# Attention scores of eight heads on eight tiles of TensorE, with the softmax, its buffers and the sums of states laid out again

## The chip, the cores and the metric

The kernel runs on one core of a Trainium2 chip. The metric is the device time of one execution in microseconds; smaller is better. A core has TensorE (PE in the rows; its weight loads are PEld), VectorE (DVE), ScalarE (ACT) and GpSimd (POOL), each of which works off its own list of instructions in order. SyncE (SP) issues most of the DMA transfers, POOL some; a queue also issues in order, so a transfer that has to wait holds up those behind it.

## The reference

```python
def _attn_ref(x, state):                     # x (8, 8, 512, 64), state (8, 8, 32, 64)
    scores = scale * np.matmul(x, state.transpose(0, 1, 3, 2))
    a = softmax(scores)                      # over the 32 states; written out, with 1e-09 in the sum
    xread = np.matmul(a, state)
    scores2 = scale * np.matmul(state, x.transpose(0, 1, 3, 2))
    a2 = softmax(scores2)                    # over the 512 tokens
    sread = np.matmul(a2, x)
    return np.concatenate([xread, sread], axis=2)

x = attn_out.transpose(0, 2, 1, 3).reshape(8 * 544, 512)
h = x @ w_in; x = (h * sigmoid(1.702 * h)) @ w_out        # 512 -> 2048 -> 512
h = x @ w_in2; out = (h * np.cos(h)) @ w_out2             # 512 -> 2048 -> 512
```

Per batch and head, 32 states and 512 tokens are scored against each other. One matrix of scores serves two softmaxes: over the states (its result reads the states for each token) and over the tokens (its result reads the tokens for each state). The 544 rows of each of the eight batches then go through two MLPs.

## The kernel before

**The first MLP.** It is worked in passes t = 0 to 6, then the tail t = 8 (the 256 rows of the states of all batches), then t = 7; a pass is one batch of 512 tokens, in 16 steps c. A step does on TensorE, in this order: `hidden(t, c)` (L499, or L507 with 12 matmuls in pass 0 and the tail; for batches 1 to 7 it is 6 matmuls against the products of states and weights, tiles `swt`), `second` of the step two before (L556, 12 matmuls into `py`), and then the pieces put into this step. ScalarE makes `t1` (Silu, L528) and `gh` (L517), VectorE `gl` (L519).

**Pieces.** While pass t runs, the attention of batch t+1 is done in pieces, and in pass 5 also the part of batch 0 that reads tokens for the states. The tuples `parts`, `first_parts` and `first_s` say which piece stands in which step; `plan` puts them into `todo`. A batch has two groups g of four heads. `scores` (L373): four matmuls of 32 columns over all 128 rows, in one bank of `ps_a`, called `psA`; the state operand `sblk` has zeros for the other head of each pair. `max_n`, `exp_n`, `norm_n` (softmax over states), `max_s`, `exp_s`, `norm_s` (over tokens), `turn_s` (four transposes into `psB`, copied to `a2T`), `sread` (16 small matmuls of `a2T` against `xN`, into `psC`), `place_s` (eight transposes on VectorE into `xs`). `ps_a` has two banks for `psA`, `psB`, `psC` and `psS`. The token tiles have one buffer per tag: one `xN_t`, two `xT_t`.

**Products of states and weights.** `sw_piece` makes them for two batches at a time: 6 matmuls into `psS` (L308), a copy to `swo` on ScalarE (L312), the remainder on VectorE (L313), and two DMAs on POOL's queue (L316) into `sw_dram`. There are 64 such pieces; `sw_steps` says in which steps. `load_sw` (L331) reads a tile `swt` of them back for one `hidden`, on SP's queue: in pass 1 and the later ones four steps ahead, for the first four steps of a pass in the last four of the pass before.

**Other work in between.** Pass 0 also decodes the weights of the first MLP on ScalarE and VectorE. Later passes decode the second MLP's first-layer weights into leaves: half a leaf unit is finished on VectorE at step 13 (L273) and stored by SP right behind it (L274, `ld<-leaf`, 1 MB). After the first MLP comes the second (L715, L725), which the change does not touch.

Of the kernel before, what the change touches and what calls it, by code (L numbers as in the profile page):

```python
# [22 lines left out]
P = 128  # L23
# [95 lines left out]
def attention_two_mlps(  # L119
# [180 lines left out]
    def sw_piece(p, f, k):  # L300

        ps = ps_a.tile([P, S], F32, name="psS", tag="psa")
        for e in range(2):
            wh, wl = wt[0, "i", 2 * f + e]
            sl = slice(k * 2 * P, (k + 1) * 2 * P)
            out_ = ps[:, e * 2 * P:(e + 1) * 2 * P]
            for i, (l, r) in enumerate(((rhi, wh), (rhi, wl), (rlo, wh))):
                nc.tensor.matmul(out_, l[:, k, :], r[:, sl], start=(e == 0 and i == 0), stop=(e == 1 and i == 2),  # L308
                                 skip_group_check=True)
        o = ep.tile([P, 4, 2, P], F32R, name="swo", tag="g")  # L310
        pv = ps.rearrange("p (c f) -> p c f", f=P)
        nc.scalar.activation(out=o[:, :, 0, :], in_=pv, func=AF.Copy)  # L312
        nc.vector.tensor_tensor(out=o[:, :, 1, :], in0=pv, in1=o[:, :, 0, :].bitcast(F32), op=ALU.subtract)  # L313
        r0 = (k % 2) * D
        for i, b in enumerate(PAIRS[p]):
            nc.gpsimd.dma_start(  # L316
                out=sw_dram[b, f][r0:r0 + D, :, k // 2, :], in_=o[i * D:(i + 1) * D].bitcast(F32).rearrange("p c h f -> p c (h f)")
            )
# [47 lines left out]
    def attn_pieces(b, g, ps_x=((ps_a, "psa"), (ps_a, "psa")), at_t="aT", at_T="T"):  # L366
# [10 lines left out]


# [4 lines left out]
        def lay_n():  # L383
            v["T"] = at.tile([P, S // NS, NS], F32, name="T", tag=at_T)
            nc.vector.transpose(out=v["T"].rearrange("p a n -> p (a n)"), in_=v["A"])
# [48 lines left out]
        def max_s():  # L434
            m2 = sm.tile([P, 1], F32, name="m2", tag="m2")
            nc.vector.tensor_reduce(out=m2, in_=v["A"], axis=AX.X, op=ALU.max)
# [3 lines left out]
        def exp_s():  # L440
            v["a2"] = at.tile([P, S], F32, name="a2", tag=f"a2{g}")
            v["s2"] = sm.tile([P, 1], F32, name="s2", tag="s2")
            nc.scalar.activation(out=v["a2"], in_=v["A"], func=AF.Exp, bias=v["b2"], scale=SCALE, accum_out=v["s2"])
# [7 lines left out]
        def turn_s():  # L451
# [3 lines left out]
            v["a2T"] = at.tile([P, S], F32, name="a2T", tag="a2T")  # L455
            nc.scalar.activation(out=v["a2T"], in_=pb, func=AF.Copy)

        def sread():
            v["C"] = ps_a.tile([P, S], F32, name="psC", tag="psa")
            n = S // P  # L460
            for c in range(n):
                for q in range(4):
                    nc.tensor.matmul(  # L463
                        v["C"][q * NS:(q + 1) * NS, :D], v["a2T"][:, c * P + q * NS:c * P + (q + 1) * NS],
# [4 lines left out]
        def place_s():  # L469
# [10 lines left out]
            scores=scores, max_n=max_n, lay_n=lay_n, most_n=most_n, exp_n=exp_n, norm_n=norm_n, sum_n=sum_n, turn_n=turn_n, high_n=high_n,  # L480
# [78 lines left out]
    def store(t, k, o=None):  # L559
        if o is None:  # L560
            pool, tag = (op, "o") if k < 2 else (ep, "g")
# [73 lines left out]
    def second_mlp(left):  # L635
# [371 lines left out]
    )  # L1007
    first_parts = (
        *parts[:3], ("norm_s 0",), ("turn_s 0", "norm_n 0"), ("high_n 0", "low_n 0"), *parts[5:],
    )  # L1010
    first_s = (
        ("scores 0",), ("scores 1", "max_s 0", "exp_s 0"), ("max_s 1", "exp_s 1", "norm_s 0"), ("turn_s 0", "norm_s 1"),
        ("sread 0", "turn_s 1", "place_s 0"), ("sread 1", "place_s 1"),
# [5 lines left out]
        ((0, 1), [(0, c) for c in (2, 4, 5, 6, 7, 7, 10, 11, 11, 12, 13, 13, 15)] + [(1, c) for c in (2, 4, 6)]),  # L1019
        ((1, 7), [(1, c) for c in (9, 10, 12, 12, 14, 15)] + [(2, c) for c in (2, 4, 6, 6, 9, 10, 12, 12, 14, 15)]),  # L1020
        ((3, 0), [(t, c) for t in (3, 4) for c in (2, 4, 6, 9, 10, 12, 14, 15)]),
        ((5, 0), [(5, c) for c in (8, 9, 12, 15)] + [(6, c) for c in (2, 4, 6, 6, 9, 10, 12, 12, 14, 15)] + [(B, 2), (B, 3)]),
# [8 lines left out]
    def run_piece(b, g, name):  # L1031
# [3 lines left out]
        nb, ng = (b, 1) if g == 0 else ((scores_of + [B])[i + 1], 0)  # L1035
        if nb < B:
            if name == "scores":
                load_xT(nb, ng)
                if g == 1:
                    load_state_t(nb)  # L1040
            if name == "sread":
                load_xN(nb, ng)

    def plan(i, t):

        pieces.update({(t + 1, g): attn_pieces(t + 1, g) for g in range(2)})
        at_step = i + (t != STATE_0)
        if t == STATE_0:
# [3 lines left out]
            at_step += len(first_s) - 1  # L1052
        for names in first_parts if t == 0 else parts:
            todo.setdefault(at_step, []).extend((t + 1, n) for n in names)
            at_step += t != STATE_0 or not names or names[0] not in ("exp_s 0", "exp_s 1")

    with tc.manual_schedule():
# [72 lines left out]
        for i, (_, t, c) in enumerate(steps1):  # L1130
# [6 lines left out]
            for u in fetches.get((t, c), ()):  # L1137
                fetch_w(*u)
            if (t, c) in todo_split:
# [15 lines left out]
            if t == 1 and 4 <= c < KF - 4 or 1 < t < B and c + 4 < KF:  # L1155
# [57 lines left out]
```

## Time and profile before

| | |
|---|---|
| time, median of 3 runs | 1408.06 us (1407.68 to 1408.36) |
| the profiled execution: time / span | 1408.07 / 1406.3 us |
| TensorE busy, share of the span | 1392.3 us, 99% |
| VectorE, ScalarE, GpSimd busy | 62%, 55%, 5% |
| mean granted TensorE clock | 0.999 of full speed |

The span runs from the first to the last instruction of the profiled execution, 1.8 us less than its own time. A line of the profile such as "L373 PE MATMUL psA<-xT_t,sblk" names line, engine, operation and tiles; x8 is a count of records, and each float32 matmul leaves two records (two passes). A row with a bracket tells how long the engine sat idle ahead of it and whose work ended the wait.

### The profile page before, as it was taken

The numbers are of one execution on the slowest core, as the hardware profiler recorded it, in microseconds if no ns is written. First come the engines' busy times: TensorE is split into PE (matmuls) and PEld (weight loads), VectorE is DVE, ScalarE is ACT, GpSimd is POOL, SyncE is SP. The second block draws the span as 40 slices with busy tenths as digits, with TensorE's granted clock in tenths as the row PEclk, the third lists the DMA queues.
The fourth block names the chain that finished last, engine by engine and source line by source line (L and its number), as shares of the span: only waits on it lengthen the run. The fifth ranks groups of instructions, "written<-read, shape, count | busy, mean of one in ns | idle before, by whom it ended". The sixth has DMA issues, their size and how long they took to land.

```text
span 1406.3 us, 19648 instructions
## 1 busy us (share of the span) xinstructions
PE 1392.3 (99%) x7134; PEld 1148.4 (82%) x7134; DVE 876.4 (62%) x1543; ACT 777.3 (55%) x1285; POOL 74.2 (5%) x124
## 2 busy tenths in 40 slices
PE   8999999999999999999999999999999999999998
PEld 6868888878887788898888888888888888888887
DVE  6764454545444555444577978677777876676664
ACT  6874644555556555455665655555455544544454
POOL 1111111211110000100000000000000000000000
PEclk9999999999999999999999999999999999999999
DMA  9756567666667564457575568555765567433353
GB/s 343 243 172 182 167 200 240 182 221 178 217 164 225 162 206 125 140 213 262 169 248 188 168 212 311 162 186 191 251 235 179 157 193 258 130 88 95 90 181 104
DMA packets 128224, 268.56 MB, mean 191 GB/s; under 512 B 17280, under 2 KB 35328, under 8 KB 126080
## 3 DMA queue, kind: packets, MB, share of 16 engines
q1 hardware_dynamic: 119024, 237.81, 51.7%
q0 software_dynamic: 8960, 29.37, 8.2%
q8 instruction: 57, 0.93, 0.3%
q14 instruction: 39, 0.32, 0.1%
q10 hardware_dynamic: 144, 0.13, 0.0%
HBM read 181.27 MB, written 85.98 MB: 190 GB/s over the span
## 4 chain that ended last, share of the span: by engine, by line
PE 96%; ACT 2%; DVE 1%; DMA 0%; issue 0%; POOL 0%; ACTq 0%; DVEq 0%; POOLq 0%
PE py L556 26%; PE bankpy L725 14%; PE bankF L725 12%; PE bankX L715 12%; PE ph L499 11%; PE bankY L715 6%; PE ph L507 4%; PE bankW L715 3%; PE psS L308 3%; PE psA L373 1%; PE psC L463 1%; PE bankX L956 1%; PE psB L454 1%; PE bankW L956 1%; PE bankY L956 1%; DMA sblk<-in_stT 0%
## 5 line engine op out<-in xcount | busy, mean ns | idle before, releaser
L556 PE MATMUL py<-gh,wo 128*128 128x512 f32 (+1 forms) x1144 | 360.1, 378 | 1.6 <-ACT wo L222 0.6
L519 DVE TENSOR_TENSOR gl<-t,gh 128x512 fp32r<-128x512 f32 (+1 forms) x143 | 96.4, 674 | 274.3 <-ACT gh L517 273.9
L556 PEld LDWEIGHTS py<-gh,wo 128*128 128x128 f32 x1144 | 211.6, 188 | 43.6 <-DVE wo L226 2.4
L725 PE MATMUL bankpy<-wo,g 128*128 128x512 f32 x864 | 219.1, 389 | 0.0
L556 PE MATMUL py<-gl,wo 128*128 128x512 f32 (+1 forms) x572 | 215.8, 377 | 0.0
L725 PE MATMUL bankF<-wo,g 128*128 128x512 f32 x768 | 194.9, 389 | 0.0
L517 ACT ACTIVATE gh<-t 128x512 fp32r<-128x512 f32 (+1 forms) x143 | 87.0, 608 | 190.8 <-PE py L556 189.6
L725 PEld LDWEIGHTS bankpy<-wo,g 128*128 128x128 f32 x864 | 161.3, 188 | 32.9
L725 PEld LDWEIGHTS bankF<-wo,g 128*128 128x128 f32 x768 | 144.0, 188 | 29.8
L499 PE MATMUL ph<-xh,swt 128*128 128x512 f32 x448 | 160.5, 399 | 0.0
L869 DVE SCALAR_TENSOR_TENSOR acc<-bankF,acc 128x512 f32<-128x512 f32 x112 | 77.4, 691 | 77.8 <-PE bankF L725 73.9
L556 PEld LDWEIGHTS py<-gl,wo 128*128 128x128 f32 x572 | 107.6, 188 | 19.9
L528 ACT ACTIVATE t<-ph 128x512 f32<-128x512 f32 (+1 forms) x144 | 82.1, 570 | 59.6 <-PE ph L499 48.8
L499 PEld LDWEIGHTS ph<-xh,swt 128*128 128x128 f32 x448 | 84.3, 188 | 27.9 <-ACT gh L517 10.1
L316 POOL DMA_DIRECT2D sd<-swo x112 | 66.8, 604 | 499.6 <-DVE swo L313 474.2
L499 PE MATMUL ph<-xl,swt 128*128 128x512 f32 x224 | 87.9, 392 | 0.0
L715 PE MATMUL bankX<-y_a,ws 128*128 128x512 f32 x336 | 85.3, 389 | 0.0
L912 ACT ACTIVATE C<-bankX 128x512 f32<-128x512 f32 x65 | 38.9, 598 | 71.8 <-PE bankX L715 71.6
L715 PEld LDWEIGHTS bankX<-y_a,ws 128*128 128x128 f32 x336 | 63.1, 188 | 13.1
L715 PE MATMUL bankX<-y_s,ws 128*128 128x512 f32 x288 | 73.1, 389 | 0.0
L699 ACT ACTIVATE r<-r 128x512 f32<-128x512 f32 (+1 forms) x72 | 43.4, 602 | 43.0 <-DVE r L697 43.0
L715 PEld LDWEIGHTS bankX<-y_s,ws 128*128 128x128 f32 x288 | 54.1, 188 | 11.2
(188 smaller groups left out, 2151.0 us busy)
## 6 DMA issues: line engine op xcount, KB each, us to landing
ws<-ld SPq DMA_DIRECT2D x256, 256.0 KB, 3.0
sd<-swo POOLq DMA_DIRECT2D x112, 256.0 KB, 3.8
swt<-sd SPq DMA_DIRECT2D x112, 256.0 KB, 4.8
rawi<-in_w_in SPq DMA_DIRECT2D x32, 512.0 KB, 7.5
rawo<-in_w_out SPq DMA_DIRECT2D x32, 512.0 KB, 6.8
ld<-leaf SPq DMA_DIRECT2D x16, 1024.0 KB, 5.3
xT_t<-in_xT SPq DMA_DIRECT2D x36, 256.0 KB, 4.0
xN_t<-in_xN SPq DMA_DIRECT2D x16, 512.0 KB, 4.5
```

The lines of the kernel that those rows point to most:

```text
L308: nc.tensor.matmul(out_, l[:, k, :], r[:, sl], start=(e == 0 and i == 0), stop=(e == 1 and i == 2), skip_group_check=True)
L316: nc.gpsimd.dma_start(out=sw_dram[b, f][r0:r0 + D, :, k // 2, :], in_=o[i * D:(i + 1) * D].bitcast(F32).rearrange("p c h f -> p c (h f)"))
L499: nc.tensor.matmul(ph, l, r, start=(g == 0 and i == 0), stop=(g == 1 and i == 2))
L507: nc.tensor.matmul(ph, w[:, f0:f0 + P], x, start=(w is wh and k == 0 and x is xk[0][0]), stop=(w is wl and k == KD - 1))
L517: nc.scalar.activation(out=gh, in_=g, func=AF.Copy)
L519: return lambda: nc.vector.tensor_tensor(out=gl, in0=g, in1=gh.bitcast(F32), op=ALU.subtract)
L528: nc.scalar.activation(out=g, in_=ph, func=AF.Silu, scale=GATE)
L556: nc.tensor.matmul(yt[k], l, r, start=(c == 0 and i == 0), stop=(c == KF - 1 and i == 2))
L699: add("ACT", 0.73 * u, lambda: nc.scalar.activation(out=R(), in_=R(), func=AF.Sin, scale=TURN), [], [rk], due - 2.7)
L715: nc.tensor.matmul(b, w[:, wl, k, :], y[:, yl, :], start=i in (0, 1, 5) and n == 0, stop=i in (3, 5, 6) and n == 5, skip_group_check=True)
L725: nc.tensor.matmul(bank(at_), l, r, start=start and i == 0, stop=stop and i == 2, skip_group_check=True)
L869: add("DVE", 0.69, lambda: nc.vector.scalar_tensor_tensor(out=flat("acc", i), in0=bank("F"), scalar=TWO_PI, in1=flat("acc", i), op0=ALU.mu ...
```

## The change

Eight edits of one design, all in the first MLP.

1. `all_scores` takes the place of the two `scores`: eight matmuls of 64 rows and 32 columns, one per head, into two banks, heads of even number in one and of odd number in the other. So group g of the softmax is now a parity of heads, `bank()` hands each group its `psA`, and `sread` picks its heads out of both turned tiles (`turned`), of which there are now two buffers (`a2T`, `a20`).
2. `parts` and `first_s` set the pieces anew. All eight heads are scored in one step; the two `exp_s` stand in one step and the two `exp_n` in another (in pass 0 too); `first_parts` is gone. In pass 0 the attention starts three steps in.
3. In pass 5, where batch 0's and batch 6's parts both stand, batch 0 has both `turn_s` in step 3, both `sread` in step 4 and both `place_s` in step 5; then `all_scores` of batch 6 in step 6.
4. `fetch` loads all four `xT_t` of the next batch, two of them into the tags `T` and `aT`.
5. `sw_piece` stores its sums in four DMAs of half the size instead of two, in another layout of `sw_dram`.
6. `sw_steps` puts 9 of these pieces into pass 0 where 13 were, and moves others.
7. In pass 1 `load_sw` loads two steps ahead (steps 6 to 13) instead of four (steps 4 to 11).
8. The stores of `py` for k = 2, 3 go through `a2T` and `a21`, the softmax's buffers, but for pass 6.

```diff
@@ -311,11 +311,13 @@
         pv = ps.rearrange("p (c f) -> p c f", f=P)
         nc.scalar.activation(out=o[:, :, 0, :], in_=pv, func=AF.Copy)
         nc.vector.tensor_tensor(out=o[:, :, 1, :], in0=pv, in1=o[:, :, 0, :].bitcast(F32), op=ALU.subtract)
-        r0 = (k % 2) * D
         for i, b in enumerate(PAIRS[p]):
-            nc.gpsimd.dma_start(
-                out=sw_dram[b, f][r0:r0 + D, :, k // 2, :], in_=o[i * D:(i + 1) * D].bitcast(F32).rearrange("p c h f -> p c (h f)")
-            )
+            for g in range(2):
+                r0 = i * D + g * NS
+                nc.gpsimd.dma_start(
+                    out=sw_dram[b, f][k * NS:(k + 1) * NS, :, g, :],
+                    in_=o[r0:r0 + NS].bitcast(F32).rearrange("p c h f -> p c (h f)"),
+                )
 
     first_sw = []
 
@@ -363,7 +365,10 @@
         nc.sync.dma_start(out=t, in_=xN[b, :, g * 256:(g + 1) * 256].rearrange("(c p) f -> p c f", p=P))
         ld[b, g, "n"] = t
 
-    def attn_pieces(b, g, ps_x=((ps_a, "psa"), (ps_a, "psa")), at_t="aT", at_T="T"):
+    banks = {}
+    turned = {}
+
+    def attn_pieces(b, g, ps_x=None, at_t="aT", at_T="T"):
         v = {}
         spare = nc.gpsimd if b == 0 and g == 1 and at_t == "a2T" else nc.vector
 
@@ -375,6 +380,19 @@
                     start=True, stop=True,
                 )
 
+        def all_scores():
+
+            for i in range(2):
+                banks[b, i] = ps_a.tile([P, S], F32, name="psA", tag="psa")
+            for k in range(KD):
+                for i in range(2):
+                    a = slice(i * D, (i + 1) * D)
+                    nc.tensor.matmul(
+                        banks[b, i][k * NS:(k + 1) * NS, :], sblk[a, k, i, :], ld[b, k // 2, k % 2][a], start=True, stop=True
+                    )
+
+        def bank():
+            return v.get("A", banks.get((b, g)))
 
         def max_n():
             lay_n()
@@ -382,7 +400,7 @@
 
         def lay_n():
             v["T"] = at.tile([P, S // NS, NS], F32, name="T", tag=at_T)
-            nc.vector.transpose(out=v["T"].rearrange("p a n -> p (a n)"), in_=v["A"])
+            nc.vector.transpose(out=v["T"].rearrange("p a n -> p (a n)"), in_=bank())
 
         def most_n():
             v["m1"] = sm.tile([P, S // NS], F32, name="m1", tag="m1")
@@ -433,14 +451,14 @@
 
         def max_s():
             m2 = sm.tile([P, 1], F32, name="m2", tag="m2")
-            nc.vector.tensor_reduce(out=m2, in_=v["A"], axis=AX.X, op=ALU.max)
+            nc.vector.tensor_reduce(out=m2, in_=bank(), axis=AX.X, op=ALU.max)
             v["b2"] = sm.tile([P, 1], F32, name="b2", tag="b2")
             nc.vector.tensor_scalar(out=v["b2"], in0=m2, scalar1=-SCALE, scalar2=None, op0=ALU.mult)
 
         def exp_s():
             v["a2"] = at.tile([P, S], F32, name="a2", tag=f"a2{g}")
             v["s2"] = sm.tile([P, 1], F32, name="s2", tag="s2")
-            nc.scalar.activation(out=v["a2"], in_=v["A"], func=AF.Exp, bias=v["b2"], scale=SCALE, accum_out=v["s2"])
+            nc.scalar.activation(out=v["a2"], in_=bank(), func=AF.Exp, bias=v["b2"], scale=SCALE, accum_out=v["s2"])
 
         def norm_s():
             nc.vector.tensor_scalar(out=v["s2"], in0=v["s2"], scalar1=EPS, scalar2=None, op0=ALU.add)
@@ -452,16 +470,17 @@
             pb = ps_a.tile([P, S], F32, name="psB", tag="psa")
             for c in range(S // P):
                 nc.tensor.transpose(pb[:, c * P:(c + 1) * P], v["a2"][:, c * P:(c + 1) * P], ident)
-            v["a2T"] = at.tile([P, S], F32, name="a2T", tag="a2T")
-            nc.scalar.activation(out=v["a2T"], in_=pb, func=AF.Copy)
+            turned[b, g] = at.tile([P, S], F32, name="a2T", tag=("a2T", "a20")[g])
+            nc.scalar.activation(out=turned[b, g], in_=pb, func=AF.Copy)
 
         def sread():
             v["C"] = ps_a.tile([P, S], F32, name="psC", tag="psa")
             n = S // P
             for c in range(n):
                 for q in range(4):
+                    s0 = c * P + (2 * g + q // 2) * NS
                     nc.tensor.matmul(
-                        v["C"][q * NS:(q + 1) * NS, :D], v["a2T"][:, c * P + q * NS:c * P + (q + 1) * NS],
+                        v["C"][q * NS:(q + 1) * NS, :D], turned[b, q % 2][:, s0:s0 + NS],
                         ld[b, g, "n"][:, c, q * D:(q + 1) * D],
                         start=(c == 0), stop=(c == n - 1),
                     )
@@ -477,7 +496,7 @@
                     )
 
         return dict(
-            scores=scores, max_n=max_n, lay_n=lay_n, most_n=most_n, exp_n=exp_n, norm_n=norm_n, sum_n=sum_n, turn_n=turn_n, high_n=high_n,
+            fetch=lambda: None, scores=scores, all_scores=all_scores, max_n=max_n, lay_n=lay_n, most_n=most_n, exp_n=exp_n, norm_n=norm_n, sum_n=sum_n, turn_n=turn_n, high_n=high_n,
             low_n=low_n, xread=xread, split_x=split_x, max_s=max_s, exp_s=exp_s, norm_s=norm_s, turn_s=turn_s,
             sread=sread, place_s=place_s,
         )
@@ -558,7 +577,7 @@
 
     def store(t, k, o=None):
         if o is None:
-            pool, tag = (op, "o") if k < 2 else (ep, "g")
+            pool, tag = (op, "o") if k < 2 else (ep, "g") if t == B - 2 else (at, ("a2T", "a21")[k - 2])
             o = pool.tile([P, sizes[t]], F32, name="o", tag=tag)
         nc.scalar.activation(out=o, in_=yt[k], func=AF.Copy, scale=1.0 / (GATE * TWO_PI))
         nc.sync.dma_start(out=y_dram[t][:, k, :], in_=o)
@@ -1000,26 +1019,23 @@
         order.write()
 
     parts = (
-        ("scores 0",), ("max_n 0", "max_s 0"), ("exp_s 0", "exp_n 0"), ("norm_s 0", "norm_n 0"), ("high_n 0", "low_n 0", "turn_s 0"),
-        (), ("sread 0", "scores 1"), ("place_s 0", "max_n 1", "max_s 1"),
-        ("exp_s 1", "exp_n 1"), ("norm_s 1", "norm_n 1"), ("high_n 1", "low_n 1", "turn_s 1"), (), ("sread 1",),
-        ("place_s 1",),
-    )
-    first_parts = (
-        *parts[:3], ("norm_s 0",), ("turn_s 0", "norm_n 0"), ("high_n 0", "low_n 0"), *parts[5:],
+        ("all_scores 0",), ("max_s 0", "max_s 1", "lay_n 0"), ("exp_s 0", "exp_s 1", "lay_n 1"),
+        ("norm_s 0", "most_n 0", "most_n 1"), ("exp_n 0", "exp_n 1"), ("turn_s 0", "norm_s 1"), ("norm_n 0",),
+        ("turn_s 1", "high_n 0", "low_n 0"), ("norm_n 1",), ("sread 0", "high_n 1", "low_n 1"), ("place_s 0", "fetch 1"),
+        ("sread 1",), ("place_s 1",),
     )
     first_s = (
-        ("scores 0",), ("scores 1", "max_s 0", "exp_s 0"), ("max_s 1", "exp_s 1", "norm_s 0"), ("turn_s 0", "norm_s 1"),
-        ("sread 0", "turn_s 1", "place_s 0"), ("sread 1", "place_s 1"),
+        ("all_scores 0",), ("max_s 0", "max_s 1", "exp_s 0", "exp_s 1"), ("norm_s 0", "norm_s 1", "fetch 1"),
+        ("turn_s 0", "turn_s 1"), ("sread 0", "sread 1"), ("place_s 0", "place_s 1"),
     )
     pieces = {}
     todo = {}
 
     sw_steps = (
-        ((0, 1), [(0, c) for c in (2, 4, 5, 6, 7, 7, 10, 11, 11, 12, 13, 13, 15)] + [(1, c) for c in (2, 4, 6)]),
-        ((1, 7), [(1, c) for c in (9, 10, 12, 12, 14, 15)] + [(2, c) for c in (2, 4, 6, 6, 9, 10, 12, 12, 14, 15)]),
-        ((3, 0), [(t, c) for t in (3, 4) for c in (2, 4, 6, 9, 10, 12, 14, 15)]),
-        ((5, 0), [(5, c) for c in (8, 9, 12, 15)] + [(6, c) for c in (2, 4, 6, 6, 9, 10, 12, 12, 14, 15)] + [(B, 2), (B, 3)]),
+        ((0, 1), [(0, c) for c in (2, 2, 6, 7, 8, 9, 11, 12, 14)] + [(1, c) for c in (0, 0, 4, 5, 6, 7, 8)]),
+        ((1, 9), [(1, c) for c in (10, 12, 14, 15)] + [(2, c) for c in (0, 4, 5, 6, 7, 9, 10, 12, 14, 15)] + [(3, 0), (3, 4)]),
+        ((3, 5), [(3, c) for c in (6, 7, 9, 10, 12, 14, 15)] + [(4, c) for c in (4, 5, 6, 7, 9, 10, 12, 14, 15)]),
+        ((5, 0), [(5, c) for c in (9, 11, 13)] + [(6, c) for c in (0, 4, 5, 6, 7, 9, 10, 12, 14, 15)] + [(B, c) for c in (2, 3, 4)]),
     )
     todo_sw = {}
     for p, (_, at_) in enumerate(sw_steps):
@@ -1033,26 +1049,28 @@
 
         i = scores_of.index(b)
         nb, ng = (b, 1) if g == 0 else ((scores_of + [B])[i + 1], 0)
+        if name == "sread" and nb < B:
+            load_xN(nb, ng)
+        nb = (scores_of + [B])[i + 1]
         if nb < B:
-            if name == "scores":
-                load_xT(nb, ng)
-                if g == 1:
-                    load_state_t(nb)
-            if name == "sread":
-                load_xN(nb, ng)
+            if name == "all_scores":
+                load_state_t(nb)
+            if name == "fetch":
+                load_xT(nb, 0)
+                load_xT(nb, 1, ("T", "aT"))
 
     def plan(i, t):
 
-        pieces.update({(t + 1, g): attn_pieces(t + 1, g) for g in range(2)})
-        at_step = i + (t != STATE_0)
+        pieces.update({(t + 1, g): attn_pieces(t + 1, g, at_T=("T", "xT0")[g]) for g in range(2)})
+        at_step = i + (3 if t == 0 else t != STATE_0)
         if t == STATE_0:
             pieces.update({(0, g): attn_pieces(0, g) for g in range(2)})
             for j, names in enumerate(first_s):
                 todo.setdefault(at_step + j, []).extend((0, n) for n in names)
-            at_step += len(first_s) - 1
-        for names in first_parts if t == 0 else parts:
+            at_step += len(first_s)
+        for names in parts:
             todo.setdefault(at_step, []).extend((t + 1, n) for n in names)
-            at_step += t != STATE_0 or not names or names[0] not in ("exp_s 0", "exp_s 1")
+            at_step += t != STATE_0 or names[0] not in ("max_s 0", "place_s 0")
 
     with tc.manual_schedule():
         seq = [("i", 0), ("i", 1)] + [(nm, j + 2 * (nm == "i")) for j in range(KF // 2) for nm in "oi" if nm == "o" or j + 2 < KF // 2]
@@ -1136,6 +1154,8 @@
             lo = gate(t, c, stores, units.get((t, c)))
             for u in fetches.get((t, c), ()):
                 fetch_w(*u)
+            if i == 0:
+                load_xT(1, 1, ("T", "aT"))
             if (t, c) in todo_split:
                 split_state(nc.vector if t else nc.gpsimd)
             if (t, c - 3) in todo_split and todo_split[t, c - 3] + 1 < len(PAIRS):
@@ -1152,7 +1172,9 @@
             if t == 0 and c == KF - 1:
                 for j in range(4, 8):
                     load_sw(1, j)
-            if t == 1 and 4 <= c < KF - 4 or 1 < t < B and c + 4 < KF:
+            if t == 1 and 6 <= c < KF - 2:
+                load_sw(t, c + 2)
+            if 1 < t < B and c + 4 < KF:
                 load_sw(t, c + 4)
             if 0 < t < B - 1 and c >= KF - 4:
                 load_sw(t + 1, c - KF + 4)
```

Three places in the order of instructions follow. The first is SP's queue around the last tiles of pass 1: `swt<-sd1_3` are tiles 12 to 15 of batch 1, `swt<-sd2_0` the first tiles of batch 2, `ld0` the half leaf stored at step 13. Before:

```order
L331 DMA swt_1632<-sd1_3_90 128x512
L331 DMA swt_1678<-sd1_3_90 128x512
L347 DMA rblk_127<-in_stT 128x4x64 x2
L331 DMA swt_1731<-sd1_3_90 128x512
L331 DMA swt_1767<-sd1_3_90 128x512
L331 DMA swt_1820<-sd2_0_91 128x512
L363 DMA xN_t_1864<-in_xN 128x4x256
L274 DMA ld0_131<-leaf0_0_1818 128x2048
```

The same place after the change:

```order
L333 DMA swt_1787<-sd1_3_90 128x512
L349 DMA rblk_127<-in_stT 128x4x64 x2
L365 DMA xN_t_1833<-in_xN 128x4x256
L333 DMA swt_1851<-sd1_3_90 128x512
L333 DMA swt_1853<-sd2_0_91 128x512
L274 DMA ld0_131<-leaf0_0_1849 128x2048
L333 DMA swt_1890<-sd1_3_90 128x512
L333 DMA swt_1892<-sd2_0_91 128x512
```

Tile 15 of batch 1 (the fourth `swt<-sd1_3`, needed by `hidden(1, 15)`) stood three transfers ahead of the leaf's store and stands now right behind it.

The second place is VectorE around step 13 of pass 1. Before:

```order
L313 TENSOR_TENSOR swo_1813<-psS_1806,swo_1813 128x4x128
L519 TENSOR_TENSOR gl_1844<-t1_1841,gh_1843 128x512
L273 TENSOR_TENSOR leaf0_0_1818<-u_1630,leaf0_0_1818 128x4x256
L519 TENSOR_TENSOR gl_1892<-t1_1889,gh_1891 128x512
L474 STREAM_TRANSPOSE xs_130<-psC_1847 32x32 x8
```

After:

```order
L313 TENSOR_TENSOR swo_1842<-psS_1835,swo_1842 128x4x128
L538 TENSOR_TENSOR gl_1877<-t1_1874,gh_1876 128x512
L493 STREAM_TRANSPOSE xs_130<-psC_1816 32x32 x8
L273 TENSOR_TENSOR leaf0_0_1849<-u_1641,leaf0_0_1849 128x4x256
L538 TENSOR_TENSOR gl_1916<-t1_1913,gh_1915 128x512
```

The eight transposes of `place_s` moved from behind the half leaf to ahead of it.

The third place is SP's queue in pass 5, where `xN_t` is loaded again for `sread 1` of batch 0 and then for batch 6; each of these loads waits until the `sread` that uses the one buffer has ended. Before:

```order
L331 DMA swt_4292<-sd5_1_104 128x512
L363 DMA xN_t_4336<-in_xN 128x4x256
L243 DMA rawi1_4_4353<-in_w_in2 128x2x512 x2
L331 DMA swt_4356<-sd5_2_105 128x512
L363 DMA xN_t_4400<-in_xN 128x4x256
```

After:

```order
L333 DMA swt_4399<-sd5_1_104 128x512
L365 DMA xN_t_4443<-in_xN 128x4x256
L365 DMA xN_t_4462<-in_xN 128x4x256
L243 DMA rawi1_4_4464<-in_w_in2 128x2x512 x2
L333 DMA swt_4467<-sd5_2_105 128x512
```

The two loads stand next to each other now, with no step between them.

## Rows read from the trace of the kernel before

**Rows 1.** Windows: length, busy us (instructions) per engine, granted clock, DMA share, GB/s.

```profile
0.00:50.00 50.00, 45.67 (x230) 33.66 (x231) 31.32 (x43) 36.73 (x46) 5.89 (x10) 1.00 1.03 351
...
200.00:450.00 250.00, 250.00 (x1385) 201.62 (x1384) 122.07 (x248) 135.31 (x213) 32.25 (x54) 1.00 0.68 204
```

**Rows 2.** Chain of pass 2, 200 to 240 us: start, us, what.

```profile
204.46 2.72 PE py L556 x12
207.18 1.00 PE psA L373 x8
208.17 1.59 PE ph L499 x6
...
217.30 1.36 PE ph L499 x6
...
236.29 0.58 PE psC L463 x32
236.87 0.86 PE psA L373 x8
```

**Rows 3.** Chain at the end of pass 1.

```profile
188.57 0.58 PE psC L463 x32
189.15 1.58 PE ph L499 x6
...
193.46 0.71 PE psS L308 x6
194.17 1.39 PE ph L499 x6
```

**Rows 4.** Timeline of PE at 18 us: two matmuls of 64 rows, two banks.

```profile
18.03 1.13 PE L425 MATMUL psX<-aT,rblk 64*128 64x512 f32 x4 [1.51 <-DVE aT L411]
```

**Rows 5.** Waits of PE up to 125 us: total, times, longest.

```profile
PE psB L454 <- DVE swo L313: 1.3, 1, 1.3
PE psS L308 <- DVE swo L313: 0.8, 1, 0.8
```

**Rows 6.** Timeline of DVE, end of pass 1.

```profile
189.33 0.69 DVE L519 TENSOR_TENSOR gl<-t,gh 128x512 fp32r<-128x512 f32 x1 [2.10 <-ACT gh L517]
189.94 1.22 DVE L273 TENSOR_TENSOR leaf<-u,leaf 128x1024 fp32r<-128x1024 f32 x1
...
194.83 1.79 DVE L474 STREAM_TRANSPOSE xs<-psC 32x32 f32<-32x32 f32 x8
```

**Rows 7.** Timeline of SP's queue, end of pass 1.

```profile
191.23 0.32 SPq L274 DMA_DIRECT2D ld<-leaf  x1
191.60 4.31 SPq L331 DMA_DIRECT2D swt<-sd  x3
```

**Rows 8.** L331, the transfers issued at 191.60 and at 192.16 us.

```profile
DMA to landing us min/median/max: 5.8/5.8/5.8
DMA to landing us min/median/max: 6.3/6.3/6.3
```

**Rows 9.** L363, 440 to 466 us: two loads of xN_t.

```profile
DMA to landing us min/median/max: 3.7/4.2/4.8
```

**Rows 10.** Timeline of ACT, pass 5, step 2.

```profile
444.27 1.28 ACT L443 ACT_TABLE_LOAD   x1
445.80 0.69 ACT L443 ACTIVATE a<-psA,b 128x512 f32<-128x512 f32 x1 [0.25 <-DVE b L438]
...
446.60 1.28 ACT L528 ACT_TABLE_LOAD   x1
...
448.52 0.63 ACT L517 ACTIVATE gh<-t 128x512 fp32r<-128x512 f32 x1
```

**Rows 11.** Timeline of PE from the start.

```profile
1.37 2.50 PE L630 MATMUL idle<-ident 128*128 128x128 f32 x10 [1.37 <-POOL ident masks.py:199]
4.01 4.07 PE L373 MATMUL psA<-xT_t,sblk 128*32 128x512 f32 x16
8.00 2.72 PE L630 MATMUL idle<-ident 128*128 128x128 f32 x22
```

## The prediction

> **What bounds the kernel now.** I read the windows first. TensorE is busy for all of 200 to 450 us, and its idle time lies at the start and in pass 0: 4.3 us in the first 50 [rows 1]. So in the middle of the first MLP, where most of the change lies, time can only come off TensorE's own list, and any wait put into that list is paid in full. Next I read the chain of waits, which there is nothing but PE rows one after the other. A plain step is 1.36 us of `hidden` and 2.72 us of `second`, 4.1 us, and each piece adds its own time [rows 2]. Then I read VectorE, ScalarE and SP's queue at the places where the change moves them.
>
> **What scores cost, and what the change takes away.** A `scores` holds the chain for 1.00 us, and the `hidden` after it takes 1.59 instead of 1.36 us, so it costs 1.00 + 0.23 = 1.23 us. A `sread` next to a `scores` is 0.58 + 0.86 + 0.23 = 1.67 us [rows 2]. A lone `sread` is 0.58 us, and the `hidden` behind it 1.58 instead of 1.39: 0.77, say 0.80 us [rows 3]. A batch needs 1.23 + 1.67 + 0.80 = 3.70 us now. After the change it is one `all_scores` and two lone `sread`. No row shows eight tiles of 64 x 32. The nearest is two matmuls of 64 rows into two banks, which end after 1.13 us for four passes [rows 4]; in series, the two passes of a `scores`, 0.5 us each, would have to come twice. I take it that they run at once, 1.23 us for `all_scores`; the upper bound is 2.23. A batch then needs 1.23 + 1.60 = 2.83, 0.87 less, and five batches (2, 3, 4, 5, 7) give 4.35 us. In pass 5 batches 0 and 6 come together: now 2 x 1.23 + 0.80 + 2 x 1.67 + 0.80 = 7.40; then 2 x 1.23 + 1.38 (two `sread` side by side, 2 x 0.58 + 0.22) + 1.60 = 5.44. That gives 1.96, together 6.3 us. If eight tiles don't run at once, these seven events cost 1.0 us more each, 7.0 in all.
>
> **Pass 0.** Here TensorE waits for VectorE and ScalarE, 1.3 and 0.8 us in the two longest waits [rows 5], behind exponentials in a step that also has weights to decode and state products to store. The change takes four state products out and moves the exponentials ahead. I expect most of these 2.1 us back, and new waits at the banks in place of some: a gain of 1.5 us, bounds -1 and +4.
>
> **New wait: tile 15 of pass 1.** Call the end of `second` in step 13 E. VectorE's `gl` starts at E + 0.76 (188.57 to 189.33) and takes 0.61 until the next can start [rows 3, 6]. Then come, new ahead of the leaf, the eight transposes, 1.79, and then the half leaf, 1.22 [rows 6]: E + 4.4. SP starts the leaf's store at once and the next transfer 0.37 us later [rows 7], so tile 15 is issued at E + 4.8. A tile issued right behind a leaf's store landed 5.8 us after its issue [rows 8]: E + 10.6. `hidden(1, 15)` would run after one step with one state product, 1.39 + 2.72 + 0.71 = 4.8 us behind E [rows 2, 3]. The wait is 5.8 us (5 to 6.5; landings behind a store were 5.8 and 6.3 [rows 8]). Now it costs nothing, because the tile is loaded four steps ahead. Tiles 12 and 14 stand behind loads of `xN_t` that wait for a `sread`; I take 0.3 us for each, 0.6 (0 to 2.6, a late load of about 1.3 each). SP's later loads slide too, but pass 2's are four steps ahead, which hides 5 us.
>
> **New waits in pass 5.** *Both sread of batch 0 in step 4.* `xN_t` has one buffer, so the second load can only be issued when the first `sread` has ended, and the second `sread` follows it with nothing between. Two such loads landed 3.7 and 4.8 us after issue, 4.2 in the middle [rows 9]: 4.2 us on the path. Now a step lies between. *Both exponentials in step 1.* ScalarE needs two table loads of 1.28, two exponentials of 0.80 (445.80 to 446.60), Silu and `gh`, 0.60 and 0.63 [rows 10]: 5.4 us in a step of 4.1, so the transposes `psB` wait about 1.3 us (0 to 3). *all_scores of batch 6 in step 6* needs both banks, which 16 transposes have to leave: E + 0.76 + 0.61 + 2 x 1.79 = E + 4.95 against 4.1 [rows 2, 3, 6]: 0.9 us (0 to 1.5). *sread 1 of batch 6 in step 15* comes one step after `sread 0`. Its load stands behind the leaf's store of step 13, and VectorE has there first `gl`, the sums over states (`norm_n`, four passes that I estimate at 0.65 each from the rows of 0.69), a remainder of a state product and the leaf. That is E + 0.76 + 0.61 + 2.6 + 0.61 + 1.22 = E + 5.8, or 5.1 us after step 14 began. The third transfer behind a leaf's store landed 7.2 us after it (191.23 to 192.16, and 6.3) [rows 7, 8]: 12.3 us, against 1.36 + 2.72 + 0.71 + 1.36 + 2.72 = 8.9 [rows 2, 3]: 3.4 us (1.5 to 4.5). The sum for pass 5 is 9.8 us.
>
> **At no cost.** POOL issues twice the DMAs, at half the size; it was busy 5% and nothing waits for it but `swt`, loaded later than the stores by some steps. The stores through `a2T` and `a21` are the same copies into idle buffers. Cover gone, a late `swo` costs under 0.5 us per step.
>
> **TensorE's clock.** Over the run the granted clock is 1.00 in every window that I read [rows 1]. But the first rows are at the lower of the two levels, 1.2 GHz: 16 score passes take 4.07 us at the start, where 8 take 1.00 later [rows 2, 11], and ten idle matmuls 2.50 us where 22 take 2.72 afterwards [rows 11]. That start lost 2.0 + 1.3 = 3.3 us. A wait of 1.5 us ahead of `psX` [rows 4] did not bring the level back down: right behind it two matmuls ran in 1.13. The new waits are longer, and I take it that the longest one, 5.8 us, costs the level once, 3.3 us (bounds: never, 0; three times, 9.9).
>
> The Trainium skill ("TensorE: Matmul & The Clock Gate", Why this matters for your kernels) warns that a wait for a transfer between bursts of matmuls puts the clock back to its lower level. By that rule all three waits above 3 us could cost it; no row of this trace has such a wait in mid-run, and only the chances of two cases below lean on it.
>
> **Sum.** -6.3 - 1.5 + 5.8 + 0.6 + 9.8 + 3.3 = +11.7 us. The profiled execution took 1408.07 us, the median is 1408.06: 1419.8 us.
>
> **Rivals.** *Some waits don't come (10%):* tile 15 or the load of `xN_t` gets there in time, one 4 to 6 us wait and the clock's loss fall away; about 1408 to 1411, within 0.2%. *None of the long ones come (11%):* the other sign, by one mechanism, transfers that land in under 4 us from when the buffer or the leaf is free and queues not in the order read: -7.8 + 2.8 (the short waits) gives 1403. For it speaks that landings differ, 3.7 to 4.8 us for two loads of one size [rows 9]; against it that even at once the leaf's data come at E + 4.4, and that the `xN_t` load has no cover at all. It decides from a tile 15 landing by E + 4.8. *The clock stays up (20%):* 1416.5. *The clock falls at all three (18%):* +6.6, 1426.4. *Eight tiles do not run at once (7%):* +7.0, 1426.8. Main case 34%.
>
> The Trainium skill ("TensorEngine Tiling (Array Packing)", Restrictions and Gotchas) says that row tiles write different PSUM banks and cannot use one bank at the same time. Grouping by parity follows that, so by the rule the tiles run together, and [rows 4] agrees with 1.13 us for two; for eight no run here shows it.
>
> **How the numbers follow.** 0.2%, 2.8 us, is about what a measurement of this kernel tells from no change. Slower: 34 + 20 + 18 + 7 = 79%; same 10%, faster 11%. The range 1408 to 1429 leaves out the faster case and little above the worst single case.
>
> **What would show it.** Right: a wait of PE at L518 for a transfer (`swt`) near 200 us of 5 to 6 us; one at L482 for `xN_t` of about 4 us early in pass 5 and another of 3 to 4 late in it; `psA` x16 in 1.0 to 1.1 us; `hidden` matmuls at half pace after a long wait. Wrong: `psA` x16 at 2 us; no wait at L518, which would mean the leaf's half is done or the tile issued earlier than read; long waits in passes 2 to 4 or 6, where I find none.

## The result

The changed kernel takes 1426.49 us (median of 4 runs, 1423.27 to 1428.09) against 1408.21 us before: a ratio of 1.0127, with a 95% interval of 1.0109 to 1.0146. It is 18 us slower. Its profiled execution took 1428.09 us, with a span of 1426.0 us and a mean granted clock of 0.992. It is the slowest of the four, so the rows below hold 1.6 us more than the median.

### The profile page after: what moved, and what is told of

Same layout as the page of the kernel before. It is cut to its first block, busy times and chain, and to the rows that moved or that the text cites. A ratio compares the mean times of both kernels' runs of the same rounds, so it can differ in the third digit from the quotient of the medians.

```text
span 1426.0 us, 19848 instructions
## 1 busy us (share of the span) xinstructions
PE 1393.6 (98%) x7134; PEld 1153.0 (81%) x7134; DVE 874.5 (61%) x1543; ACT 775.0 (54%) x1283; POOL 124.2 (9%) x236
## 4 chain that ended last, share of the span: by engine, by line
PE 93%; DMA 3%; ACT 2%; DVE 1%; issue 1%; SPq 0%; ACTq 0%; DVEq 0%
PE py L575 25%; PE bankpy L744 14%; PE bankF L744 12%; PE bankX L734 12%; PE ph L518 11%; PE bankY L734 6%; PE ph L526 3%; PE psS L308 3%; PE bankW L734 3%; DMA xN_t<-in_xN 1%; PE psC L482 1%; DMA rawi<-in_w_in 1%; PE psA L390 1%; PE bankX L975 1%; PE bankW L975 1%
## 5 line engine op out<-in xcount | busy, mean ns | idle before, releaser
L317 POOL DMA_DIRECT2D sd<-swo x224 | 117.7, 528 | 473.4 <-DVE swo L313 444.9
```

The lines of the kernel that those rows point to most:

```text
L317: nc.gpsimd.dma_start(out=sw_dram[b, f][k * NS:(k + 1) * NS, :, g, :], in_=o[r0:r0 + NS].bitcast(F32).rearrange("p c h f -> p c (h f)"),)
```

## The profile after

The waits of TensorE over the whole span of the changed kernel come first (engine, tile and line, whose work ended the wait: us in total, times, longest).

```profile
PE psC L482 <- DMA xN_t<-in_xN: 9.3, 2, 5.6
PE ph L518 <- DMA swt<-sd: 6.6, 1, 6.6
PE psB L472 <- DVE s L464: 2.1, 1, 2.1
...
PE ph L518 <- ACT gh L536: 0.7, 1, 0.7
```

Before, the longest wait behind 125 us was 0.2 us. Now four of over 2 us stand there, at the places that the prediction named. The last line, 0.7 us, stands at `hidden(1, 12)` (at 176.80 us) and is the wait for tile 12: the tile was issued at 171.71 and landed 5.0 us later, 0.1 us ahead of the `hidden`. The profile names `gh`, which ended just after the tile had landed. But in e1_tile15 below the same `hidden` starts at 175.63, before its `gh` ends at 175.77, so it is not `gh` that it needs; in all eight other kernels below it waits 0.6 to 1.2 us there, and the profile names the tile. The longest wait is tile 15 of pass 1. The chain of waits around it, 180 to 230 us (start, us, what):

```profile
184.02 2.73 PE py L575 x12
...
187.51 0.69 DVE gl L538
...
189.93 1.24 DVE leaf L273
...
191.22 0.32 SPq L274
...
191.59 6.55 DMA swt<-sd
...
198.27 2.90 PE ph L518 x6
201.17 2.89 PE py L575 x12
...
213.70 1.02 PE psA L390 x16
214.72 1.58 PE ph L518 x6
...
219.04 1.36 PE ph L518 x6
```

Read from top to bottom, the chain leaves TensorE at the end of `second` (186.75), goes through `gl`, the transposes and the half leaf on VectorE, then SP, then the tile's transfer, and comes back 11.5 us later; for the first 4.9 us of these TensorE still had the step between to do. The `hidden` behind the wait takes 2.90 us where a later one takes 1.36: the matmuls run slowly at first. The last rows show `all_scores`: 16 passes in 1.02 us, and 1.58 instead of 1.36 us for the `hidden` behind it, 1.24 us in all. That is what four heads cost before (1.23 [rows 2]).

The chain of pass 5, 428 to 480 us and 505 to 535 us, in two answers:

```profile
444.28 2.98 DMA yd<-o
...
453.15 0.63 PE psB L472 x4
453.78 2.37 PE ph L518 x6
456.14 3.35 PE py L575 x12
459.50 0.63 PE psC L482 x32
...
460.14 3.44 DMA xN_t<-in_xN
...
463.72 0.76 PE psC L482 x32
464.48 2.86 PE ph L518 x6
467.34 2.89 PE py L575 x12
...
474.31 0.97 PE psA L390 x2
...
475.36 1.09 PE psA L390 x14
```

```profile
514.37 8.54 DMA xN_t<-in_xN
...
523.05 1.08 PE psC L482 x32
524.13 2.86 PE ph L518 x6
526.99 3.75 PE py L575 x12
```

Here are the wait at `psB`, the two loads of `xN_t`, and between them the banks: `psA` takes 0.97 us for two passes and 1.09 for the other 14, 1.1 us more than its 1.02. At the top stands one thing that the prediction did not have: `yd<-o`, the DMA of a store, on the way to the exponential. ScalarE's timeline shows what it costs there:

```profile
447.36 0.69 ACT L461 ACTIVATE a<-psA,b 128x512 f32<-128x512 f32 x1 [1.02 <-DMA yd<-o]
```

The clock, by stretches of 4 us (length, busy us of PE, PEld, DVE, ACT, POOL, granted clock, DMA share, GB/s):

```profile
186.00:190.00 4.00, 4.00 (x19) 3.15 (x18) 2.37 (x10) 1.23 (x2) 0.60 (x2) 1.00 0.57 182
...
194.00:198.00 4.00, 0.00 (x0) 0.00 (x0) 0.00 (x0) 0.00 (x0) 1.60 (x4) 0.56 0.89 214
198.00:202.00 4.00, 3.73 (x10) 3.02 (x11) 0.00 (x0) 0.60 (x1) 0.00 (x0) 0.59 0.46 178
202.00:206.00 4.00, 4.00 (x21) 3.36 (x21) 1.18 (x2) 1.23 (x2) 0.00 (x0) 1.00 0.26 66
...
452.00:456.00 4.00, 3.48 (x15) 2.77 (x16) 1.54 (x5) 1.20 (x2) 0.00 (x0) 0.74 0.90 343
...
464.00:468.00 4.00, 4.00 (x36) 3.09 (x25) 0.00 (x0) 0.60 (x1) 0.00 (x0) 0.57 0.52 141
...
524.00:528.00 4.00, 4.00 (x16) 3.15 (x10) 0.00 (x0) 0.60 (x1) 0.00 (x0) 0.50 0.85 281
```

Behind each of the three waits for a transfer the granted clock lies near half, that is at 1.2 of 2.4 GHz for most of the stretch; behind `psB` it is 0.74.

**Where 20 us went.** The profiled executions differ by 20.0 us, their spans by 19.7. Against the kernel before, pass 0 ends 1.3 us earlier, once the four state products moved out of it are put back in (`hidden(1, 0)` starts at 118.13 instead of 122.24, and 4 x 0.71 us are owed). Tile 15 costs 6.6 and tile 12 0.7; pass 5 costs 2.1 + 3.6 + 1.1 + 5.6 = 12.4. Then come the slow matmuls, each against its like at full speed (0.44 for `psB`, 0.58 for `psC`, 1.36 for `hidden`, 1.38 behind `psB` and 1.58 behind `psC`, 2.72 for `second`): behind tile 15 1.54 + 0.17; behind `psB` 0.19 + 0.99 + 0.63; behind the first `xN_t` 0.18 + 1.28 + 0.17; behind the second 0.50 + 1.28 + 1.03; 8.0 us together. About 0.6 of these 8.0 are not the clock: the first matmuls behind any wait take longer at a granted clock of 1.00 too (`hidden` 1.62 us behind the wait for tile 12, 0.26 more than 1.36; `psB` 0.63 in e2_same_xN and e6_store4, where 0.44 is usual; `psC` 0.65 behind a wait of 1.4 us in e5_all, 0.07 more than 0.58, twice). That leaves 7.4 for the clock.

The scores bring 0.85 us in pass 2 and 0.89 in pass 3 (`hidden(t, 2)` is 6.55, 5.70 and 4.81 us late in passes 2, 3 and 4, with one state product owed at each). If every batch brings what was forecast, they bring 6.3, and the sum is 7.3 + 12.4 + 8.0 - 6.3 - 1.3 = 20.1. That this meets 20.0 is in part luck. From `hidden(1, 0)` to the tail, with waits and slow matmuls taken out, 5.5 us are left for the scores. And the tail's first `hidden`, which before was spread over 2.86 us because GpSimd's `xtail` came late, takes 1.66 now: 1.2 us that nobody forecast. With these two, 7.3 + 12.4 + 8.0 - 5.5 - 1.2 - 1.3 = 19.7, the difference of the spans; the 5.5 is what was left over, not a term read by itself.

## The experiments

The theory: each long wait has its own cause in the order of instructions, and each costs its length and a stretch of slow clock on top; the new form of the scores itself does what it should. The rival for each is named with it.

**e1_tile15.**

```diff
-            if t == 1 and 6 <= c < KF - 2:
+            if t == 1 and 6 <= c < KF - 3:
                 load_sw(t, c + 2)
+            if t == 1 and c == KF - 4:
+                load_sw(t, KF - 1)
```

> The changed kernel with one edit: tile 15 of batch 1 is read in step 12 of pass 1, ahead of batch 2's first tile and of the half leaf's store, instead of in step 13 behind it. Theory (the tile is late because its read stands in SP's queue behind the leaf's store, which waits for VectorE): the wait of 6.6 us at L518 is gone, and with it the slow matmuls behind it (1.5 us in the next hidden, 0.2 in the next second): 8.3 us less than the changed kernel, about 1418. Rival (the sums of states themselves reach memory too late, since their pieces stand in steps 5 to 8): the wait stays or comes up at tile 14 or 15, under 2 us gained.

It took 1418.98 us (ratio to the kernel before 1.0078, 1.0061 to 1.0095), 7.5 us less than the changed kernel. Of TensorE's waits from 125 to 230 us one is left:

```profile
175.63 0.47 PE L518 MATMUL ph<-xh,swt 128*128 128x512 f32 x1 [0.59 <-DMA swt<-sd]
```

The wait was the place in the queue. The sums of states are in memory in time, so the rival is out. The 0.6 us stand at `hidden(1, 12)`: it is the wait for tile 12, as in the changed kernel. The gain is not the wait and its slow stretch alone: the clock fell in other places here (behind `psB` the `hidden` took 2.08 us instead of 2.37; behind the first `xN_t` `psC`, `hidden` and `second` took 1.08, 2.86 and 3.75 instead of 0.76, 2.86 and 2.89).

**e2_same_xN.**

```diff
-        if name == "sread" and nb < B:
+        if name == "sread" and (nb, ng) == (0, 1):
+            ld[0, 1, "n"] = ld[0, 0, "n"]
+        elif name == "sread" and nb < B:
             load_xN(nb, ng)
```

> The changed kernel without the second load of xN_t for batch 0: its second sread uses the token tile of the first, so the output of four heads of batch 0 is left wrong. Theory (one buffer, and a load with nothing to cover it): the wait of 3.6 us at L482 early in pass 5 is gone, and with it 1.6 us of slow matmuls behind it: 5.2 us less, about 1421. Rival (the second sread would wait as long for its turned tile, copied on ScalarE): the wait stays and changes its releaser.

1420.29 us (1.0088, 1.0073 to 1.0103), 6.2 less. The two `sread` run as one piece, with nothing slow behind them (chain, 452 to 470 us):

```profile
452.94 0.63 PE psB L472 x4
453.57 1.38 PE ph L518 x6
...
457.67 1.03 PE psC L482 x64
458.70 1.58 PE ph L518 x6
```

So the load alone was the wait; the turned tile is there. The rows also show what was not looked for: the wait of 2.1 us at `psB` is the same in this run, but the `hidden` behind it takes 1.38 us, not 2.37. The clock did not fall here. Between the two profiled executions that is 1.6 us which the expectation did not count.

**e3_sread6.**

```diff
+        if t == STATE_0:
+            turned_first = (*parts[:8], ("norm_n 1", "sread 0"), ("high_n 1", "low_n 1"), *parts[10:])
-        for names in parts:
+        for names in turned_first if t == STATE_0 else parts:
```

> The changed kernel with sread 0 of batch 6 one step earlier in pass 5 (step 13, with norm_n 1), so that the next load of xN_t is put into SP's queue ahead of the half leaf's store. Theory (the load is late because it stands behind the leaf): the wait of 5.6 us at L482 at the end of pass 5 is gone, with 2.8 us of slow matmuls behind it: 8.4 us less, about 1418. Rival (the load is late because it waits for its buffer, two steps are too few for it): 2 to 4 us of the wait stay.

1419.30 us (1.008, 1.0065 to 1.0095), 7.2 less. At the end of pass 5 the second `sread` now follows `second` at once (chain, 495 to 520 us):

```profile
507.91 0.58 PE psC L482 x32
...
517.59 0.58 PE psC L482 x32
518.18 1.58 PE ph L518 x6
```

The edit does two things at once: it puts the load ahead of the half leaf, and it gives it a step more. The time to landing tells them apart. In the changed kernel the leaf's store is issued at 513.50 and the load at 514.37, and it lands 8.5 us later; here (issued at 508.56) it takes

```profile
DMA to landing us min/median/max: 3.8/3.8/3.8
```

A plain step is 4.1 us, so by this landing one step would have been about enough (an estimate). It was not the buffer that made the load late, but its place in the queue, behind the half leaf and next to four loads of `xT_t`.

**e4_stores.**

```diff
-            pool, tag = (op, "o") if k < 2 else (ep, "g") if t == B - 2 else (at, ("a2T", "a21")[k - 2])
+            pool, tag = (op, "o") if k < 2 else (ep, "g")
```

> The changed kernel with edit 8 undone: all four stores of py go through the tag g as before the change. Theory (in pass 5 the second exp_s writes the buffer a21 out of which a store has just begun, and so waits 1.0 us for that DMA): the wait of ScalarE for yd is gone and the wait of PE at psB falls from 2.1 to about 1.1 us; 1.0 us less, and 1.6 more if the shorter wait leaves TensorE's clock up: 1424 to 1425.5. Rival (ScalarE's list of two table loads, two exponentials and four stores is what is late, or the tag g makes a wait of its own): no change or slower.

1432.34 us (1.0173, 1.0158 to 1.0188): 5.9 us slower than the changed kernel, a miss. The half that was expected came true: `psB` waits 1.0 us. But a new wait stands in the list of TensorE's waits, and the chain of pass 1, 120 to 140 us, tells whose it is:

```profile
PE py L575 <- ACT o L582: 4.5, 3, 2.5
...
PE psB L472 <- DVE s L464: 1.0, 1, 1.0
```

```profile
125.82 3.80 DMA sd<-swo
...
129.72 0.61 ACT o L582
...
130.35 3.11 DMA yd<-o
...
133.54 0.61 ACT o L582
...
134.19 1.65 PE py L575 x3
```

The two state products that edit 6 puts into step 0 hold the buffers of tag `g`, so the third store waits for their DMAs and the fourth for the third's. Behind this wait, 2.5 us at TensorE, the granted clock was 0.61 from 134 to 138 us and the `hidden` took 2.02. Edit 8 is what makes room for edit 6; the prediction took it for a copy that costs and saves nothing.

**e6_store4**, its narrower form.

```diff
-            pool, tag = (op, "o") if k < 2 else (ep, "g") if t == B - 2 else (at, ("a2T", "a21")[k - 2])
+            pool, tag = (op, "o") if k < 2 else (ep, "g") if t in (STATE_0 - 1, B - 2) else (at, ("a2T", "a21")[k - 2])
```

> The changed kernel with the stores of pass 4 alone through the tag g. Theory (edit 8 helps in passes 1 to 4, where the tag g is taken by the state products of step 0, and hurts only in pass 5, where both exponentials follow at once): no wait of ScalarE's stores in passes 1 to 4; in pass 5 the wait at psB falls from 2.1 to 1.0 us and the clock stays up behind it, 2.5 to 2.8 us less than the changed kernel, about 1423.7. Rival (any store through g has to wait in pass 5 too): no gain.

1425.62 us (1.0125, 1.0111 to 1.0139), 0.9 us less where 2.5 to 2.8 were expected: by the medians a miss. The wait at `psB` is 1.0 us, no store waits in pass 5, and the clock is 1.00 from 445 to 457 us. The two profiled executions differ by 2.6 us, but the changed kernel's is the slowest of its four, and its runs spread by 4.8. So the rows show that the DMA of the store costs 1.0 us of the wait; that the clock's part comes off in the median is not shown.

**e7_by_bank.**

```diff
-            for k in range(KD):
-                for i in range(2):
+            for i in range(2):
+                for k in range(KD):
```

> The changed kernel with the eight score matmuls put out bank by bank (four heads of even number, then four of odd) instead of in turn. Theory (TensorE runs tiles together wherever their rows and columns differ, whatever the order of issue): psA x16 still 1.02 us. Rival (only neighbours in the list run together, and the second bank's start behind the first's): about 1.5 to 2.0 us at each of the seven events, 3.5 to 7 us more.

One run, 1426.67 us. In the chain of pass 2, 205 to 240 us:

```profile
213.68 1.02 PE psA L390 x16
214.70 1.58 PE ph L518 x6
```

The same 1.02 us; the order within the eight does not matter.

**e5_all** takes the waits away together: the edits of e1, e3 and e6, and batch 0's part one step earlier with its two `sread` a step apart.

```diff
-        ("turn_s 0", "turn_s 1"), ("sread 0", "sread 1"), ("place_s 0", "place_s 1"),
+        ("turn_s 0", "turn_s 1"), ("sread 0",), ("sread 1", "place_s 0"), ("place_s 1",),
...
-        if t == STATE_0:
+        if t == STATE_0 - 1:
             pieces.update({(0, g): attn_pieces(0, g) for g in range(2)})
             for j, names in enumerate(first_s):
-                todo.setdefault(at_step + j, []).extend((0, n) for n in names)
-            at_step += len(first_s)
+                todo.setdefault(i + KF - 1 + j, []).extend((0, n) for n in names)
+        if t == STATE_0:
+            at_step += len(first_s) - 1
```

> The changed kernel with its long waits taken away together: tile 15 read in step 12 of pass 1; batch 0's part begun one step earlier (its scores in the last step of pass 4), its two sread in steps 3 and 4 of pass 5; sread 0 of batch 6 in step 13, ahead of the half leaf's store; the stores of pass 4 through the tag g; one state product moved from step 15 to step 11 of pass 4. Theory (the scores and pass 0 do bring what they were predicted to, 6.3 and 1.2 us, and only the waits and the slow clock behind them turn it over): no wait of over 1 us after pass 0, no slow matmuls, 1400.5 to 1402, faster than the kernel before. Rival (the scores bring less, or new waits take the place of these): 1405 or more.

1405.05 us (0.998, 0.9971 to 0.9989): faster than the kernel before, but 3 us short of what was expected. It is the rival that came, by its second half: new waits in place of the old ones. Two waits over 1 us are left behind pass 0:

```profile
PE py L575 <- ACT o L582: 2.4, 1, 2.4
...
PE psC L482 <- DMA xN_t<-in_xN: 1.4, 1, 1.4
```

The first is ScalarE's list early in pass 5, 429.6 to 438.0 us: two table loads, both exponentials, half a leaf and four stores. The second is the load of `xN_t`, which one step does not cover here: it landed 5.5 us after its issue.

**e8_earlier** starts batch 0's part one step earlier still, where ScalarE has neither the half leaf nor the stores, and gives the load two steps. Against e5_all (one state product, moved from step 14 to step 13 of pass 4 with it, is left out here):

```diff
-        ("turn_s 0", "turn_s 1"), ("sread 0",), ("sread 1", "place_s 0"), ("place_s 1",),
+        ("turn_s 0", "turn_s 1"), ("sread 0",), ("place_s 0",), ("sread 1",), ("place_s 1",),
...
-                todo.setdefault(i + KF - 1 + j, []).extend((0, n) for n in names)
+                todo.setdefault(i + KF - 2 + j, []).extend((0, n) for n in names)
...
-            at_step += len(first_s) - 1
+            at_step += len(first_s) - 2
```

> The fifth kernel with batch 0's part begun one step earlier still: scores in step 14 of pass 4, exponentials in step 15, where ScalarE has neither half a leaf nor stores, the two sread in steps 2 and 4 of pass 5, and two state products moved into steps 11 and 13 of pass 4. Theory (the 2.4 us at the second of step 2 come from ScalarE's list of exponentials, half a leaf and stores, the 1.4 us at sread 1 from a load with one step to land): both waits gone, 3.5 to 3.9 us less than the fifth kernel, about 1401.3. Rival (the table loads are late wherever the two exponentials stand together, or the stores through g wait): 1 us or less gained.

1401.48 us (0.9953, 0.9939 to 0.9967), 6.5 us less than the kernel before and 3.6 less than e5_all, as expected; both waits are gone. From 100 us on its windows show next to no idle TensorE and a full clock:

```profile
100.00:430.00 330.00, 329.37 (x1886) 269.44 (x1885) 168.09 (x339) 176.26 (x278) 86.67 (x165) 1.00 0.66 205
430.00:520.00 90.00, 89.33 (x547) 71.17 (x546) 46.33 (x104) 47.39 (x76) 4.20 (x8) 1.00 0.58 186
```

## Why the prediction was right, point by point

- **What bounds it.** Right. Every wait put into TensorE's list behind pass 0 was paid in full; e1, e2 and e3 each gave back a wait and its slow matmuls (7.5, 6.2 and 7.2 us for 8.3, 5.2 and 8.4 expected). The differences of about 1 us are of the size by which the clock's falls at `psB` and at the first `xN_t` differed in these runs.
- **Scores.** Right: 1.24 us for eight heads where 1.23 was taken; the upper bound, 2.23, is out. The gain of 0.87 per batch measured 0.85 and 0.89. The case in which eight tiles do not run at once is out. Over all batches about 5.5 of the 6.3 us are left when waits and slow matmuls are taken out.
- **Pass 0.** 1.3 us for 1.5, but not by the mechanism given, and so by luck. The waits behind `psB` and `psS` did fall, from 2.8 to 0.4 us. But the loads of `xT_t` (1.6) and the weights `wo` (2.5 for 1.1) took nearly all of it back, not the banks: TensorE's idle time up to `hidden(1, 0)` is 7.6 us, and was 7.8. What fell is its work: batch 1's scores, 0.87 us, stand in pass 0 too, and the prediction counted them nowhere. The figure also differs from one execution to the next: in the eight other kernels, whose pass 0 is the same (in e7_by_bank but for the order of the scores), it is 1.2 to 2.9 us, and the difference is there by step 2, at 20 us.
- **Tile 15.** The mechanism, step by step, as predicted; 6.6 us for 5.8, because the tile landed 6.55 us after its issue, not 5.8. Tiles 12 and 14 were priced at 0.3 each; tile 12 waited 0.7 and tile 14 not at all.
- **Pass 5.** The loads: 3.6 for 4.2 and 5.6 for 3.4. The second was mis-sized by its landing, 9.4 us behind the leaf's store (513.50 to 522.91) instead of 7.2; the leaf's store was issued as worked out, 5.1 us into step 14. The 7.2 was read from an `swt` tile (128x512), half the size of this load (128x4x256), and with no loads of `xT_t` behind it; which of the two made it late was not tried. Banks 1.1 for 0.9.
- **psB.** 2.1 for 1.3. The step that failed is "The stores through `a2T` and `a21` are the same copies into idle buffers": in pass 5 the second exponential writes `a21` while the store's DMA still reads it, and 1.0 us of the wait is that (e6: 2.1 to 1.0). In passes 1 to 4 the same edit saves more than it costs here (e4).
- **Clock.** The largest error, and one of number: 3.3 us for one fall, where four were seen, 7.4 us (8.0 with the slower first matmuls). A fall cost 1.5 to 1.6 us, once 2.7, nearer to half of the 3.3 read from the start, where 6.6 us of matmuls had run slowly. That the start was at the lower level was worked out from the paces alone, since the clock column of [rows 1] reads 1.00 there; behind the waits the same half pace stands beside a column of 0.50 to 0.59. The rule cited from the Trainium skill ("TensorE: Matmul & The Clock Gate", Why this matters for your kernels) held for all three waits for a transfer. The fourth fall, behind 2.1 us at `psB`, the prediction did not consider.
- **The sum.** 11.7 us were forecast; the medians differ by 18.3, the profiled executions by 20.0. The gains were 8.0 us for 7.8, with 1.2 at the tail that was not forecast; the waits were 3.5 us too small (19.7 for 16.2) and the slow matmuls 4.7. The case "the clock falls at all three" (1426.4), which the prediction gave 18%, is nearest to what came. That its figure meets the median (1426.49) is luck: it has three falls at 3.3 where four cheaper ones came, and waits that are too small by 3.5.
- **A sum that does not come out.** The case "some waits don't come" takes one wait and the clock's 3.3 off 1419.8. With tile 15 that gives 1410.7, with the first `xN_t` 1412.3; the stated 1408 to 1411 lies too low.

## What to carry to other kernels

When pieces of work are moved, the gain on the bottleneck engine is easy to count; what decides is each transfer whose distance to its user shrinks. Follow each one through its queue: what stands ahead, what that waits for, and when the buffer is free. Where TensorE would idle for several microseconds, add the slow stretch behind it, and read a buffer as idle only once the DMA out of it has landed. Here the same change with four such distances mended went from 18 us slower to 6.5 us faster.

## What the runs showed of the hardware

Wherever TensorE waited 3.6 us or more in mid-run, in any kernel here, the granted clock fell behind the wait. The price was not fixed: behind the same wait of 3.6 us for `xN_t` the slow matmuls cost 1.6 us in the changed kernel and 2.8 in e1_tile15. At 2 to 2.5 us it fell in some profiles and not in others. Behind the same wait of 2.1 us at `psB` it fell in the changed kernel (0.74, `hidden` 2.37 us) and in e1_tile15 (0.71, 2.08), and stayed at 1.00 in e2_same_xN, e3_sread6 and e7_by_bank (1.38 to 1.39). A wait of 2.5 us in e4_stores brought it down, one of 2.4 us in e5_all did not. What else decides it was not tried. It may be a part of why the changed kernel's runs spread over 4.8 us where the kernel before spreads over 0.8; only one of them was traced, so that is not shown, and pass 0 alone differs by 1.6 us between the profiles.

Eight score matmuls of 64 rows and 32 columns took 1.02 us, as long as four of 128 rows took before (1.00), in turn or bank by bank. A load of `xN_t` landed 8.5 us after its issue behind the leaf's store and with four loads of `xT_t` after it in the queue, and 3.8 us after it in e3_sread6, with nothing ahead of it in the queue.
